# Attention and routed experts on one core: products without a reader ahead of the first expert's row transposes, and a new order for its first products

## The chip, the cores and the metric

The kernel runs on one core of one Trainium2 chip. The core has five engines with queues of their own: PE (TensorE, matrix products and transposes), DVE (VectorE), ACT (ScalarE), POOL (GpSimd) and SP (which here only issues transfers). An engine takes its instructions strictly in the order of its queue; a wait at the head holds back everything behind it. The profile also has PEld, the loading of a product's stationary operand, which overlaps PE. The metric is the device time of one execution in microseconds (us), less is better; the time before is the median of three runs.

## The reference

Two layers in a row. The first is an attention that adds a coarse part (queries, keys and values averaged by four, softmax over all) and a local part (softmax over the seven nearest keys). The second sends each of the 4608 tokens to one of 8 experts, greedily by score, 576 tokens to each, and applies that expert's two-layer network:

```
order = np.argsort(-flat)                 # all token-expert scores, highest first
for idx in order:
    tok, e = (int(idx) // E, int(idx) % E)
    if assigned[tok] >= 0 or counts[e] >= cap:
        continue
    assigned[tok] = e
    counts[e] += 1
...
for e in range(E):
    mask = assigned == e
    h = np.maximum(x[mask] @ w1[e], 0.0)  # 576 x 512 by 512 x 1024
    out[mask] = h @ w2[e]                 # 576 x 1024 by 1024 x 512
```

## The kernel before, in words

The attention comes first and takes about the first 292 us. It writes its rows x to memory and leaves the scores of all tokens on the chip. Then the experts follow one after the other, in the order in which they fill up. For each of them there are two parts.

*The routing* (class Routing, `phase`) finds the next expert to fill up and the list of its 576 tokens. It is a chain of comparisons on DVE (L703), counts on PE (L733, L744, L749) and small steps on DVE between them; `emit` turns the result into the list `idx`. Its last products are the 18 of L994; the list itself is written by four DVE instructions at L1004. The routing of the next expert is worked into the products of the current one: its setup on DVE (L810 to L856) is followed by the first comparison and count, and so on.

*The expert* (class Experts) loads its weights (`weights`, L1036), splits each of them into a high and a low 16-bit half (`split`: ACT makes the high one at L1052, DVE the low one at L1054), and gathers the 576 rows of x by five indirect transfers, issued by POOL (L1069): four row tiles of 128 rows and one of 64. For the first expert (and the second) each row tile is transposed on PE with four instructions (`piece`, L1078) into a bank of PSUM named pX, of which there are two; ACT copies it out as the high half of `xt` (L1081) and DVE subtracts to get the low half (L1082), which frees the bank. For the later experts a DMA transposes.

`mlp` does the products. The 1024 hidden columns are cut into eight blocks f of 128. For each of them the rows are cut in two: columns 0 to 255 of `xt` (row tiles 0 and 1) and columns 256 to 575 (row tiles 2, 3 and 4, 320 columns). Either part takes 12 products: four slices d of the depth, each with high by high, high by low and low by high halves. The order of the three matters here: the first product of a part only needs the high half of `xt`, the second needs the low half, which DVE makes last. Both parts of a block go to one tile pH in PSUM (two banks), of which there are two in turn; ACT takes it out with the rectifier (L1119), DVE makes the low half (L1122), and then the bank pair is free for block f + 2. The second layer's products (L1135) follow.

The order on each queue comes from the framework's planner. It takes instructions by priority as they become ready in its own estimate of times, so it may put a product of block 1 ahead of one of block 0 that still waits. The program can force an order: `issue_after` and `behind_` (L708) write an edge between two instructions of the same engine that sets their order in the queue and adds no wait. The routing and the first expert's row tiles are traced with the highest priority.

The queue of PE around the change, as the profile has it: 18 products of L994, the transposes of tiles 0 and 1, one product each of blocks 0 and 1, the transposes of tiles 2 and 3, ten products of block 0, the transposes of tile 4, the last of block 0's first part and most of block 1's first part, then block 0's 12 products of 320 columns and the rest of block 1's first part.

Of the kernel before, what the change touches and what calls it, by code (L numbers as in the profile page):

```python
# [6 lines left out]
F32 = mybir.dt.float32  # L7
# [1000 lines left out]
class Experts:  # L1008
    def __init__(self, ctx, tc, x_dram, w1, w2, out, ident, ps, raw):
        self.tc, self.nc, self.x, self.w1, self.w2, self.out, self.ps = tc, tc.nc, x_dram, w1, w2, out, ps  # L1010
        self.raw = raw
        self.wt = ctx.enter_context(tc.tile_pool(name="wt", bufs=2))
        self.wk = ctx.enter_context(tc.tile_pool(name="mwk", bufs=2))
        self.ident = ident
        self.sc, self.second, self.sent = [], {}, None

    def weights(self, ei, late):

        nc = self.nc
        raw = []  # L1020

        def load(eng, ii):
            e = eng.value_load(ei[:1, :1], min_val=0, max_val=E - 1)
            for i in ii:
                t = self.raw.tile([128, 2048], F32, name="nat")
                if i < 2:
                    src = self.w1[bass.DynSlice(e, 1), 256 * i:256 * i + 256].rearrange("o (a p) f -> p (o a) f", p=128)
                    dst = t.rearrange("p (a f) -> p a f", a=2)
                else:
                    src = self.w2[bass.DynSlice(e, 1), 512 * i - 1024:512 * i - 512].rearrange(  # L1030
                        "o (a p) d -> p (o a) d", p=128)
                    dst = t.rearrange("p (a d) -> p a d", a=4)
                n = dst.shape[1] // 2
                for a in ((0, n), (n, 2 * n)) if late and i < 2 else ((0, 2 * n),):
                    with self.tc.issue_after(self.sent.ins) if i > 1 and self.sent else nullcontext():
                        eng.dma_start(dst[:, a[0]:a[1]], src[:, a[0]:a[1]])  # L1036
                raw.append(t)

        load(nc.sync, (0, 1) if late else (0, 1, 2, 3))
        return (raw, lambda: load(nc.gpsimd, (2, 3))) if late else raw  # L1040

    def split(self, raw, first):

# [16 lines left out]
    def gather(self, idx, first):  # L1060


        nc = self.nc
        xt = self.wk.tile([128, 2, 4, CAP], F16, name="xt")
# [9 lines left out]
        def piece(c):  # L1074
            s0, n = SL[c]
            p = self.ps.tile([128, 4, 128], F32, name="pX", bufs=2)
            for d in range(4):
                self.turned = nc.tensor.transpose(p[:, d, :n], xgs[c][:n, 128 * d:128 * d + 128], self.ident[:n, :n])  # L1078
            hi, lo = xt[:, 0, :, s0:s0 + n], xt[:, 1, :, s0:s0 + n]
            with self.tc.high_priority():  # L1080
                nc.scalar.activation(hi, p[:, :, :n], AF.Copy, scale=XM)  # L1081
                nc.vector.scalar_tensor_tensor(lo, p[:, :, :n], XM, hi, op0=OP.mult, op1=OP.subtract)  # L1082
# [10 lines left out]

        return xt, piece if first else piece_dma

    def mlp(self, w, xt, idx, in1, in2):
        nc = self.nc

        ht = self.wk.tile([128, 8, 2 * CAP], F16, name="ht", bufs=1)
        CUT = ((0, 256), (256, CAP))  # L1100
        for f in range(8):
            p = self.ps.tile([128, 2, 512], F32, name="pH", bufs=2)
            seq = [(d, a, b) for d in range(4) for a, b in ((0, 0), (0, 1), (1, 0))]
            for s, (s0, s1) in enumerate(CUT):
                for j, (d, a, b) in enumerate(seq):
                    mm = nc.tensor.matmul(p[:, s, :s1 - s0], w[d][a][:, 128 * f:128 * f + 128], xt[:, b, d, s0:s1],  # L1106
                                          start=j == 0, stop=j == len(seq) - 1)
            if f == AFT:
                aft = mm
            with self.tc.high_priority():  # L1110
                los = []
                for i, (n0, n1) in enumerate(((0, 256), (256, 320))):
                    q = p[:, :, n0:n1] if i == 0 else p[:, 1:, n0:n1]
                    m = q.shape[1]
                    s0 = 0 if i == 0 else 512
# [9 lines left out]
        for c, (s0, n) in enumerate(SL):  # L1125
            p = self.ps.tile([128, 512], F32, name="pX", bufs=2)
# [3 lines left out]
            seq = [(h0, f, b) for f in range(8) for h0, b in ((s0, 0), (s0, 1), (lo, 0))]  # L1130
# [25 lines left out]
GET = {-1: (0, 1), 0: (2, 3), 1: (4,)}  # L1156
GET0 = {3: (0, 1), 4: (2, 3, 4)}
BEHIND = ((1, 6), (2, 10))


def moe_attention(tc, q, k, v, wg, w1, w2, cst, out):
    nc = tc.nc
    with ExitStack() as top:
# [6 lines left out]
        ro = Routing(top, tc, lg, cst)  # L1170
# [6 lines left out]
        with ExitStack() as ctx:  # L1177
# [3 lines left out]
            with tc.high_priority(TOP):  # L1181
                idx, (raw, rest) = ro.phase(False, True, lambda ei: ex.weights(ei, True))
                w, split = ex.split(raw, True)
                xt, piece = ex.gather(idx, True)
                with tc.issue_after(ex.fetched.ins):
                    rest()
                with tc.issue_after(ro.done.ins):
                    for k in range(4):
                        split(k)
                for c in range(5):  # L1190
                    piece(c)
            w1st = split
            for i in range(E):
# [32 lines left out]
                                    split(2 * c)  # L1226
                                    split(2 * c + 1)

                ex.mlp(w, xt, idx, in1, in2)
                if i == 0:  # L1230
                    for at, mms in zip(BEHIND, ro.late):
                        for mm in mms:
                            ro.behind_(mm, ex.second[at])
# [58 lines left out]
```

## Time and profile before

| | |
|---|---|
| median of 3 runs | 787.49 us (786.25 to 787.55) |
| the profiled execution's own time | 784.24 us |
| its span, from the first to the last instruction | 782.3 us |
| mean granted TensorE clock | 0.942 of full |
| PE busy | 676.3 us (86%) |
| DVE busy | 562.3 us (72%) |
| ACT busy | 331.8 us (42%) |
| POOL busy | 242.1 us (31%) |
| L1106, the first layer's products, high half of the weights: 1024, 287 ns each in the mean | 197.1 us |
| L1106, low half of the weights: 512, 287 ns each | 146.5 us |

The profile is of one execution, whose own time lies 3.25 us below the median. Its span is divided by engine, line and tile. [...] A transpose on PE is a matmul with the identity and stands under the line that issues it. PEclk is the clock that TensorE was granted, as a share of full speed: in the 40 slices of the page it is below full at nine places, the longest of them being slices 15 and 16 (about 293 to 332 us), where it is half. The share of busy time is a mean over stages; the change lies in one stage of some 20 us, so it is read from the windows and the timeline there.

### The profile page before, as it was taken

The page shows a single profiled execution, that of the slowest core. Times are in us where ns is not written, and L with a number is a line of the kernel's source. Part 1 is how long each engine was busy: PE and PEld are TensorE (multiplying, and loading weights), DVE is VectorE, ACT ScalarE, POOL GpSimd, SP SyncE. Part 2 cuts the span into 40 slices and gives each one's busy share as a digit, 9 for nine tenths or more (in the row PEclk, how much of TensorE's full clock was granted, in tenths as well). Part 3 has the DMA queues.
Part 4 walks back from the last instruction along what each step waited for, and adds up shares of the span by engine and source line. Part 5 has one row for each costly group of instructions (what it writes and reads, how often), then busy time and mean ns, then how long its engine had stood idle before and what let it go on. Part 6 is the DMA issues. An engine that isn't in the chain of part 4 may idle for free.

```text
span 782.3 us, 21188 instructions
## 1 busy us (share of the span) xinstructions
PE 676.3 (86%) x8565; PEld 467.8 (60%) x8565; DVE 562.3 (72%) x1679; ACT 331.8 (42%) x631; POOL 242.1 (31%) x274
## 2 busy tenths in 40 slices
PE   6588888986988873399899999999989999999994
PEld 4577677775777662265466466466457476574752
DVE  7778878987797887886968979798959645171210
ACT  3357576673766450341623426134225234262210
POOL 9263544735355450300510412121230402201001
PEclk9689999998999995599999999999999999999997
DMA  9949979797999850620714565562742673804001
GB/s 262 217 121 246 249 197 268 199 271 195 260 229 206 204 184 12 182 96 27 277 34 163 168 137 208 102 238 61 227 171 108 131 267 75 216 2 101 22 27 34
DMA packets 148133, 125.00 MB, mean 160 GB/s; under 512 B 92228, under 2 KB 122436, under 8 KB 148036
## 3 DMA queue, kind: packets, MB, share of 16 engines
q1 hardware_dynamic: 140656, 102.12, 49.2%
q0 software_dynamic: 6432, 20.98, 8.9%
q8 instruction: 68, 1.11, 0.6%
q10 hardware_dynamic: 948, 0.55, 0.3%
q14 instruction: 29, 0.24, 0.1%
HBM read 95.30 MB, written 21.23 MB: 149 GB/s over the span
## 4 chain that ended last, share of the span: by engine, by line
PE 33%; issue 26%; DVE 22%; DMA 7%; ACT 5%; POOL 3%; SPq 2%; another core or an unknown queue 1%; ACTq 0%; POOLq 0%; DVEq 0%
PE pH L1106 8%; PE pX L1135 6%; PE g L476 2%; POOL out_dram L1144 2%; DMA vw<-in_v_dram 2%; DVE cmp L703 2%; PE g L292 2%; PE pR L733 2%; PE g L325 2%; PE g L436 2%; PE g L373 1%; DVE x L407 1%; PE g L454 1%; DVE wl L1054 1%; DVE xt L499 1%
## 5 line engine op out<-in xcount | busy, mean ns | idle before, releaser
L1106 PE MATMUL pH<-xt,wh 128*128 128x256 f16 (+1 forms) x1024 | 197.1, 287 | 0.7 <-ACT xt L1081 0.7
L1135 PE MATMUL pX<-wh,ht 128*128 128x512 f16 (+1 forms) x640 | 182.2, 383 | 1.9 <-DVE xt L1082 1.9
L1106 PE MATMUL pH<-xt,wl 128*128 128x320 f16 (+1 forms) x512 | 146.5, 287 | 0.0
L1135 PEld LDWEIGHTS <-ht 128*128 128x128 f16 (+1 forms) x960 | 82.1, 101 | 91.5 <-issue 7.8
L1144 POOL DMA_INDIRECT out_dram<-y,idx x40 | 44.4, 1111 | 286.4 <-ACT y L1141 262.4
L1135 PE MATMUL pX<-wl,ht 128*128 128x512 f16 (+1 forms) x320 | 119.1, 384 | 0.0
L1106 PEld LDWEIGHTS <-wh 128*128 128x128 f16 x1024 | 97.8, 98 | 26.7 <-issue 3.5
L1119 ACT ACTIVATE ht<-pH 128x512 f16<-128x512 f32 (+1 forms) x128 | 45.5, 408 | 123.3 <-PE pH L1106 123.3
L1054 DVE SCALAR_TENSOR_TENSOR wl<-nat,wh 128x512 f16<-128x512 f32 x128 | 84.7, 683 | 2.7 <-ACT wh L1052 0.5
L1069 POOL DMA_INDIRECT xg<-x_dram,idx x40 | 47.1, 1178 | 105.2 <-DVE idx L1004 34.0
L1141 ACT ACTIVATE y<-pX 128x512 f32<-128x512 f32 (+1 forms) x40 | 23.7, 593 | 130.5 <-PE pX L1135 78.5
L1122 DVE SCALAR_TENSOR_TENSOR ht<-pH,ht 128x512 f16<-128x512 f32 (+1 forms) x128 | 52.5, 450 | 33.8 <-ACT ht L1119 33.3
L1052 ACT ACTIVATE wh<-nat 128x1024 f16<-128x1024 f32 x64 | 66.6, 1056 | 9.9 <-DMA nat<-in_moe_w_dram 9.9
L1106 PEld LDWEIGHTS <-wl 128*128 128x128 f16 x512 | 50.1, 98 | 11.9
L465 ACT COPY pt<-g 64x512 f32<-64x512 f32 x72 | 41.8, 580 | 33.7 <-PE g L454 32.5
L292 PE MATMUL g<-ident,nat 128*128 128x128 f32 x256 | 41.1, 288 | 13.7 <-DMA nat<-in_q_dram 8.7
L476 PE MATMUL g<-vw,pt 128*64 128x65 f32 x1152 | 45.0, 231 | 5.6 <-issue 3.0
L1143 DVE SCALAR_TENSOR_TENSOR y<-pX,y 64x512 f32<-64x512 f32 x8 | 5.5, 693 | 59.8 <-ACT y L1141 59.8
L476 PEld LDWEIGHTS g<-vw,pt 128*64 128x64 f32 x1152 | 39.9, 144 | 11.6 <-ACT pt L465 5.6
L278 ACT COPY kt<-g 64x512 f32<-64x512 f32 (+1 forms) x56 | 35.2, 629 | 19.4 <-PE g L292 11.6
L278 ACT COPY qz<-g 64x512 f32<-64x512 f32 (+1 forms) x52 | 33.0, 635 | 21.2 <-PE g L292 20.6
L265 POOL TENSOR_TENSOR gtmp<-qz 64x576 f32<-64x576 f32 x28 | 32.0, 1144 | 30.8 <-DVE kdt L268 29.2
(219 smaller groups left out, 1189.5 us busy)
## 6 DMA issues: line engine op xcount, KB each, us to landing
nat<-in_moe_w_dram SPq DMA_DIRECT2D x28, 1024.0 KB
vw<-in_v_dram SPq DMA_DIRECT2D x136, 96.0 KB
up<-up_dram SPq DMA_DIRECT2D x36, 256.0 KB
x_dram<-x SPq DMA_DIRECT2D x36, 256.0 KB
nat<-in_q_dram SPq DMA_DIRECT2D x16, 512.0 KB
nat<-in_k_dram SPq DMA_DIRECT2D x16, 512.0 KB
nat<-in_v_dram SPq DMA_DIRECT2D x14, 512.0 KB
up_dram<-xu SPq DMA_DIRECT2D x16, 128.0 KB
```

The source lines that it names most:

```text
L278: self.nc.scalar.copy(out, in_)
L292: nc.tensor.transpose(p[:, a, :, fp], src[:, 4 * hh + 2 * a + s, 2 * fp:2 * fp + 2].rearrange("p f d -> p (f d)"), self.ident)
L465: self.nc.scalar.copy(out, in_)
L476: nc.tensor.matmul(o[64 * i:64 * i + 64, 65 * h:65 * h + 65], pt[:, 2 * g + i, h].rearrange("p b q -> p (b q)"), self.vw[u % 4][:, i, 4 * ...
L1052: nc.scalar.activation(hi, r, AF.Copy, scale=sc)
L1054: nc.vector.scalar_tensor_tensor(lo[:, a:a + LOP], r[:, a:a + LOP], sc, hi[:, a:a + LOP], op0=OP.mult, op1=OP.subtract)
L1069: self.fetched = nc.gpsimd.indirect_dma_start(out=xg[:n], out_offset=None, in_=self.x, in_offset=bass.IndirectOffsetOnAxis(ap=idx[:n, c:c ...
L1106: mm = nc.tensor.matmul(p[:, s, :s1 - s0], w[d][a][:, 128 * f:128 * f + 128], xt[:, b, d, s0:s1], start=j == 0, stop=j == len(seq) - 1)
L1119: last = nc.scalar.activation(hi, q, AF.Relu)
L1122: nc.vector.scalar_tensor_tensor(lo, q, 0.0, hi, op0=OP.max, op1=OP.subtract)
L1135: mm = nc.tensor.matmul(p[o:o + m], ht[:, f, h0:h0 + m], w[4 + f // 2][b][:, 512 * (f % 2):512 * (f % 2) + 512], start=j < parts, stop=j > ...
L1144: i = nc.gpsimd.indirect_dma_start(out=self.out, in_=y[:n], in_offset=None, out_offset=bass.IndirectOffsetOnAxis(ap=idx[:n, c:c + 1], axis=0))
```

## The change

Three edits, all for the first expert only.

1. `spin` issues 24 products right behind the last product of L994 (an `issue_after` edge). Each multiplies a tile of ones (128 by 128, 16 bit) with a table of 288 columns that the routing keeps on the chip, and writes to a pH tile that nobody reads.
2. In `mlp` the first parts (256 columns) of blocks 0 and 1 are issued ahead of the second part of block 0, so that the first 24 products need row tiles 0 and 1 alone. For the other blocks, and the other experts, the order is as it was.
3. Order edges put the transposes of row tile 2 behind product 6 of those 24 (counted from 0), those of tile 3 behind product 12, those of tile 4 behind product 18.

```diff
+    def spin(self, a, b):
+        p = self.ps.tile([128, 2, 512], F32, name="pH", bufs=2)
+        n = b.shape[1] * b.shape[2]
+        for _ in range(SPIN):
+            self.nc.tensor.matmul(p[:, 0, :n], a, b.rearrange("p e t -> p (e t)"), start=True, stop=True)
+
...
+            self.turns.append([])
             for d in range(4):
                 self.turned = nc.tensor.transpose(p[:, d, :n], xgs[c][:n, 128 * d:128 * d + 128], self.ident[:n, :n])
+                self.turns[-1].append(self.turned)
...
-    def mlp(self, w, xt, idx, in1, in2):
+    def mlp(self, w, xt, idx, in1, in2, first=False):
...
+        seq = [(d, a, b) for d in range(4) for a, b in ((0, 0), (0, 1), (1, 0))]
+
+        def product(f, p, s):
+            s0, s1 = CUT[s]
+            for j, (d, a, b) in enumerate(seq):
+                mm = nc.tensor.matmul(p[:, s, :s1 - s0], w[d][a][:, 128 * f:128 * f + 128], xt[:, b, d, s0:s1],
+                                      start=j == 0, stop=j == len(seq) - 1)
+                self.products.append(mm)
+            return mm
+
+        ph = {}
         for f in range(8):
-            p = self.ps.tile([128, 2, 512], F32, name="pH", bufs=2)
-            seq = [(d, a, b) for d in range(4) for a, b in ((0, 0), (0, 1), (1, 0))]
-            for s, (s0, s1) in enumerate(CUT):
-                for j, (d, a, b) in enumerate(seq):
-                    mm = nc.tensor.matmul(p[:, s, :s1 - s0], w[d][a][:, 128 * f:128 * f + 128], xt[:, b, d, s0:s1],
-                                          start=j == 0, stop=j == len(seq) - 1)
+            for z in (0, 1) if first and f == 0 else () if first and f == 1 else (f,):
+                ph[z] = self.ps.tile([128, 2, 512], F32, name="pH", bufs=2)
+                product(z, ph[z], 0)
+            p = ph.pop(f)
+            mm = product(f, p, 1)
...
+TURN = (6, 12, 18)
+SPIN = 24
...
+                with tc.issue_after(ro.late[-1][-1].ins):
+                    ex.spin(ro.one, ro.codes)
...
-                ex.mlp(w, xt, idx, in1, in2)
+                ex.mlp(w, xt, idx, in1, in2, i == 0)
                 if i == 0:
+                    for at, mms in zip(TURN, ex.turns[2:5]):
+                        for mm in mms:
+                            ro.behind_(mm, ex.products[at])
```

More of the change, by code (lines that the diff above doesn't have):

```diff
@@ L1014, in __init__ @@
         self.ident = ident
-        self.sc, self.second, self.sent = [], {}, None
+        self.sc, self.second, self.sent, self.products, self.turns = [], {}, None, [], []
     def weights(self, ei, late):
```

## The prediction

> **What bounds the kernel now.** I read the stage table first (busy us of PE, PEld, DVE, ACT, POOL, each with its count; then granted clock, DMA share, GB/s), then the chain of waits, then the clock.
>
> ```profile
> span 782.3 us, 21188 instructions
> 320.20:326.10 5.90, 0.00 (x0) 0.00 (x0) 5.68 (x21) 3.17 (x3) 3.28 (x3) 0.50 0.57 208
> 337.50:350.70 13.20, 12.60 (x121) 8.80 (x120) 11.85 (x30) 6.66 (x13) 0.00 (x0) 1.00 0.01 2
> 350.70:385.00 34.30, 34.30 (x256) 18.40 (x256) 27.47 (x109) 11.18 (x19) 6.38 (x6) 1.00 0.44 157
> ```
>
> After the first expert's list of tokens PE is idle for 5.90 us, at half clock. From 350.70 to 385.00 it has no gap, so what is won or lost at 350.70 reaches the end. From 337.50 to 350.70 both PE (12.60 of 13.20) and DVE (11.85) are nearly full. The chain between, in order of time (start, length, what; pieces of 0.05 us and less left out):
>
> ```profile
> 322.21 3.92 DMA xg<-x_dram,idx
> 326.18 1.13 PE pX L1078 x4
> 327.33 0.60 ACT xt L1081
> 327.93 1.16 issue
> 329.09 0.61 ACT xt L1081
> 329.74 0.58 PE pH L1106 x2
> 330.32 1.79 PE pX L1078 x8
> 332.10 2.03 PE pH L1106 x10
> 334.13 0.41 PE pX L1078 x4
> 334.56 0.39 ACT xt L1081
> 334.98 0.42 DVE xt L1082
> 335.41 0.09 DVE h L829
> ...
> 337.02 0.84 DVE cmp L703
> 337.90 0.42 PE pR L733 x10
> ```
>
> Row tile 0 is transposed when its gather lands (326.13), tile 1 when its own lands (327.93). Two products follow ACT's copy of tile 1; DVE's subtraction frees the rest, and the planner has filled that wait with tiles 2 and 3. That subtraction ends at 329.72 + 0.69 = 330.41:
>
> ```profile
> 329.72 0.69 DVE L1082 SCALAR_TENSOR_TENSOR xt<-pX,xt 128x512 f16<-128x512 f32 x1 [1.06 <-ACT xt L1081]
> ```
>
> Behind tile 4's subtraction stands DVE's setup for the second expert, whose comparison ends at 337.85.
>
> **The clock.** Rows of the granted clock (length, PE busy, count, clock, DMA share, GB/s). Each of these holds a change:
>
> ```profile
> 292.75:293.00 0.25, 0.00 (x0) 0.87 0.00 0
> 333.80:333.90 0.10, 0.10 (x3) 0.53 1.09 451
> 388.50:389.00 0.50, 0.00 (x0) 0.51 0.00 0
> 391.50:392.00 0.50, 0.50 (x6) 0.58 0.81 319
> ```
>
> A row's mean clock places the change in it: 0.87 in 292.75 to 293.00 is a fall at 292.94; the others are at 333.89 (rise), 388.51 (fall) and 391.92 (rise). The distances are 40.95, 54.62 and 3.41 us: 12, 16 and 1 times 3.413. So the clock is decided on a grid of 3.413 us. Six stretches of that grid, in the same columns:
>
> ```profile
> 289.52:292.93 3.41, 1.63 (x32) 1.00 0.39 144
> 74.48:77.89 3.41, 1.80 (x42) 1.00 0.30 92
> 770.80:774.21 3.41, 1.31 (x14) 1.00 0.20 77
> 327.07:330.48 3.41, 2.09 (x10) 0.50 0.68 197
> 388.51:391.92 3.41, 2.89 (x14) 0.50 0.22 74
> 47.17:50.58 3.41, 3.41 (x40) 0.50 0.00 0
> ```
>
> I laid that grid over the whole span. It falls nine times; the busiest stretch ahead of a fall is 1.63 of 3.41 (48%), the idlest after which it stayed full is 1.80 (53%). It rose after 2.89 (85%), not after 2.09 (61%), and once not after a full one. I take: below about half busy it falls; above some 61 to 85% it rises.
>
> **The change, part by part.**
>
> ```profile
> 318.61 1.42 PE L994 MATMUL pR<-r,ohl 128*64 128x72 bf16 x18 [2.85 <-DVE r L981]
> 332.11 0.42 PE L1106 MATMUL pH<-xt,wl 128*128 128x256 f16 x1
> 332.75 0.42 PE L1106 MATMUL pH<-xt,wl 128*128 128x256 f16 x1
> 336.11 0.30 PE L1106 MATMUL pH<-xt,wl 128*128 128x320 f16 x1
> 336.52 0.30 PE L1106 MATMUL pH<-xt,wl 128*128 128x320 f16 x1
> 337.17 0.38 PE L1106 MATMUL pH<-xt,wh 128*128 128x256 f16 x2
> 337.39 0.27 PE L1106 MATMUL pH<-xt,wl 128*128 128x256 f16 x1
> 386.50 0.66 PE L1078 MATMUL pX<-ident,xg 128*128 128x128 f32 x4 [0.98 <-ACT y L1141]
> 389.03 0.58 PE L1135 MATMUL pX<-wh,ht 128*64 128x512 f16 x1 [1.87 <-DVE xt L1082]
> ```
>
> Prices from start to start: a product of 256 columns is 0.64 / 3 = 0.213 us at half clock (three from 332.11 to 332.75) and 0.22 / 2 = 0.11 at full (two from 337.17 to 337.39). One of 320 is 0.41 / 3 = 0.137 at full. Four transposes are 1.13 at half (chain) and 0.65 at full (386.50).
>
> *The 24 products* have 288 columns, so 0.24 us at half, 0.122 at full. They follow L994's last product (320.03). Were the clock never to rise they end at 320.05 + 5.76 = 325.81, before the gather at 326.13: hidden in the idle 5.90 us. Without that cover they would cost 2.9 to 5.8 us. They write a pH buffer that nobody reads; its next user is PE itself, so no wait comes of it. On the recorded grid the stretch 320.24 to 323.65 is full: the clock rises at 323.65, with 15 done; the nine left take 1.1 us, to 324.75.
>
> *What of the clock is left.* Stretch 323.65 to 327.07 holds 1.1 + 0.65 (tile 0) = 1.75, 51%: between 48 and 53%, undecided; I take it as kept. Tile 1 is gated by its gather and gains 1.13 − 0.65 = 0.48: the first two products start at 329.26, the rest at 329.94 (the subtraction, 0.48 earlier). Stretch 327.07 to 330.48 then holds 0.65 + 0.3 + 0.54 = 1.5, 44%: **the clock falls again at 330.48**, just as the products become dense, and rises at 333.89 as before. A fall one step earlier only takes the 0.48 away.
>
> *The moved transposes*, on PE. By 330.48 some 7 products are done. At half clock follow one more (0.28), tile 2 (1.13), five products (1.07) and most of tile 3 by 333.89; then its end (0.1), six products (0.65), tile 4 (0.41, to 335.05) and five products (0.54): 335.6. Tile 4's subtraction lasts ACT's 0.39 and DVE's 0.42 with about 0.1 of gaps, to 336.0, and the second product of 320 columns waits for it, some 0.3. Eleven of them (1.5) end at 337.5. Before, the same 36 products and five transposes ended at 337.39 + 0.11 = 337.50. So PE's sum is 0.0: the 0.48 goes into waits that tiles 2 and 3 filled before.
>
> *ACT and DVE.* The moved transposes issue no DMA; ACT's copies and DVE's subtractions move with them on those queues. ACT has room (1.16 us of issue between two copies in the chain). On DVE it matters: tile 4's subtraction ends at 336.0 instead of 335.40, and what is queued behind it (L829 to the comparison, then PE's count L733) would be 0.6 late. If the planner, seeing tile 4 later, puts the setup ahead of it, that chain comes up to 0.6 early instead. At the end of the stage DVE has slack:
>
> ```profile
> 350.70 0.17 DVE L751 TENSOR_REDUCE nj<-pR 128x1 f32<-128x8 f32 x1 [0.87 <-PE pR L749]
> ```
>
> It waits 0.87 us for PE there, so a late DVE costs only through the waits that it makes for PE before: between 0 and +0.6. The subtotal is −0.6 to +0.6.
>
> *The grid of other executions.* Nothing in one execution ties the grid to the kernel's start. Shifted by −0.8, +0.8, +1.7 and +2.3 us, the same working has the clock fall again at 326.3, 327.9, 328.8 and 325.9, and PE ends its 36 products 0.6, 2.1, 0.4 and 0.6 us later than before on the same grid. With the recorded grid's 0.0 the middle one of the five is +0.6. PE's waits in the next stage (13.20 − 12.60 = 0.60) can take up a little of it; I take **+0.5 us**. On the profiled execution's own 784.24 (span 782.3 and 1.94 around it) that is 784.7. This execution is 3.25 below the median of 787.49; on the median it is 788.0. The case's own range is −0.6 (recorded grid, DVE early) to +2.1.
>
> [...]
>
> **The rivals.**
>
> *The clock stays full* (a lower limit than half, or a luckier grid). Then the first two products start at 329.26, five or so follow from 329.94 to 330.6, tile 2 to 331.27, products, tile 3 to 332.46, products, tile 4 from 333.1 to 333.5, the 24 end at 334.0, a wait to 334.45 for the subtraction, and the 320s end at 336.0: PE −1.5, DVE −0.95. (Tile 4's gather is there: tile 3's had landed by about 331.2, amid the eight transposes of the chain, and two gathers landed 1.8 us apart, 326.13 and 327.93.) The change is between these, −1.25: 786.2. For it: after the spin no gap exceeds 1.4 us, and the undecided stretch lies at the limit. Against it: nine falls of nine below 48%, one of them at 38% (1.31 of 3.41).
>
> *Slower: the rise comes a grid step late.* Before, tiles 2 and 3 keep PE full from 329.74 on; now PE must pass seven products before tile 2, and idles until the subtraction (about 0.3 us at half clock). It decides where the grid puts a boundary near 331.3: before, that stretch (327.87 to 331.28) holds 1.13 + 1.54 = 2.67, 78%; now 1.13 + 0.4 + 0.83 = 2.4, 70%. Both lie between 61 and 85%; with the limit between them, the half clock lasts 3.41 us longer, which costs PE up to 1.7, and with the 0.3 lost and DVE's chain behind it +2.0: 789.5. For it: the rows leave the limit open just there. Against it: it needs a grid in about a third of the positions.
>
> *It does nothing*: the planner finds no place for the products ahead of tile 0, or orders the later transposes as now. Then 787.5. Against it: both are bound by written order edges.
>
> **How the numbers follow.** 0.2% is 1.57 us, about what a measurement of this kernel can tell from no change. Chances: forecast 0.47, clock stays full 0.32, late rise 0.16, nothing 0.05. New orders on DVE and ACT farther on, which no row shows, can add some to either side. Faster: half of the second (its own bound of −1.5 is just short), 0.16, and an eighth of the first, 0.06: 0.22. Slower: four fifths of the third, 0.13, and a sixth of the first, 0.08: 0.21. Same: 0.57. The range reaches from a little beyond the clock kept (−2.1, 785.4) to the late rise (+2.1, 789.6).
>
> **What would show it.** Right: clock 1.00 from about 323 to 326, 0.50 again somewhere between 326 and 333, products of 0.213 us among the transposes. Wrong: a clock of 1.00 from 324 to 338 (the first rival), a tile 0 that starts after 326.3 (the spin costs), the first comparison for the second expert ending more than 1 us from 337.85 (the order on DVE changed), or a shift at 337 that is not the shift at 385.

## The result, and the profile after

The changed kernel takes 785.09 us (median of 22 runs, 782.21 to 796.54) beside 788.59 for the kernel before (22 runs on the same chip). The ratio is 0.9943, with a 95% interval of 0.9924 to 0.9963: it is faster by some 4.5 us. (The ratio is that of the mean times, without the slow run of 796.54 us, 1.8% above the fastest.) The profiled execution took 783.15 us. Forecast were 788.0 and a range from 785.4 to 789.6.

From the page of the changed kernel, the head, the busy times and one of the DMA queues (packets, MB, share of 16 engines):

```profile
span 781.4 us, 21233 instructions
PE 681.5 (87%) x8589; PEld 471.6 (60%) x8589; DVE 560.8 (72%) x1679; ACT 332.0 (42%) x631; POOL 245.5 (31%) x274
q8 instruction: 68, 1.11, 0.6%
```

PE is busy 5.2 us longer than before (676.3) and still the kernel is shorter. The queue of instructions is as before, 68 packets; it will matter below.

The timeline of PE in the changed kernel (start, length, work, count, idle time ahead and its releaser). New line numbers: 1046 the added products, 1085 the transposes (1078 before), 1114 and 1153 the products of the first and second layer (1106, 1135).

```profile
320.19 1.42 PE L994 MATMUL pR<-r,ohl 128*64 128x72 bf16 x18 [2.85 <-DVE r L981]
321.54 5.07 PE L1046 MATMUL pH<-codes,one 128*128 128x288 bf16 x24
327.84 0.66 PE L1085 MATMUL pX<-ident,xg 128*128 128x128 f32 x4 [1.23 <-DMA xg<-x_dram,idx]
329.42 0.66 PE L1085 MATMUL pX<-ident,xg 128*128 128x128 f32 x4 [0.92 <-DMA xg<-x_dram,idx]
330.76 0.38 PE L1114 MATMUL pH<-xt,wh 128*128 128x256 f16 x2 [0.69 <-issue]
332.14 1.04 PE L1085 MATMUL pX<-ident,xg 128*128 128x128 f32 x8
385.41 0.66 PE L1085 MATMUL pX<-ident,xg 128*128 128x128 f32 x4 [0.36 <-ACT y L1159]
387.94 0.38 PE L1153 MATMUL pX<-wh,ht 128*64 128x512 f16 x1 [1.87 <-DVE xt L1090]
```

The added products end 1.23 us ahead of tile 0, which the gather releases 7.65 us after the first L994 product (327.84 − 320.19; before 7.57): they are hidden. The clock, in windows of the changed kernel (length, busy us of PE, PEld, DVE, ACT, POOL with counts; granted clock, DMA share, GB/s):

```profile
325.50:325.75 0.25, 0.25 (x4) 0.14 (x3) 0.25 (x2) 0.19 (x1) 0.13 (x1) 0.84 0.00 0
325.58:328.99 3.41, 1.69 (x12) 1.01 (x10) 3.41 (x7) 1.49 (x2) 2.76 (x3) 1.00 0.54 154
328.99:332.41 3.42, 1.95 (x15) 1.53 (x16) 2.54 (x6) 0.74 (x2) 3.11 (x4) 1.00 0.72 193
571.34:574.75 3.41, 1.40 (x17) 1.01 (x18) 1.15 (x3) 0.59 (x1) 1.30 (x1) 1.00 0.53 193
```

The first row places the rise at 325.58, in the added products, and in this execution the clock stays full until 574.75: the first whole stretch of the grid behind the rise held 1.69 of 3.41 us, half. The last row is the stretch ahead of that later fall, 41% busy. The chain of waits of the changed kernel has the first comparison for the second expert far earlier than before:

```profile
335.40 0.74 DVE cmp L703
336.19 0.41 PE pR L733 x10
```

It ends 15.95 us after the first L994 product (336.14 − 320.19), where it ended 19.25 after it before (337.86 − 318.61). On DVE the setup for the second expert now stands ahead of the subtractions of tiles 2 to 4, not behind that of tile 4.

Where did the time go? Marks of the two profiles, in us after the first L994 product, worked out from the timelines of PE:

```
                                       before   after   gained
second layer of expert 1 starts         44.0     42.4     1.6
second layer of expert 1 ends           74.6     70.5     2.5 more
PE ends                                453.5    451.0    -1.6 more
```

The first stage gains 1.6, the next 2.5, and the rest gives 1.6 back. The clock fall at 574.75 (6.8 us at half clock) lies in that rest; a second profile of the change (e4 below), without a fall there, needs 377.3 us for it, where the kernel before needs 378.9 (453.5 − 74.6). So some 1.6 us were gained there too, where no line of the program changed.

### The profile page after: what moved, and what is told of

Read it like the earlier page. It is cut to its first block, busy times and chain, and to the rows that moved or that the text cites. A ratio compares the mean times of both kernels' runs of the same rounds, so it can differ in the third digit from the quotient of the medians.

```text
span 781.4 us, 21233 instructions
## 1 busy us (share of the span) xinstructions
PE 681.5 (87%) x8589; PEld 471.6 (60%) x8589; DVE 560.8 (72%) x1679; ACT 332.0 (42%) x631; POOL 245.5 (31%) x274
## 3 DMA queue, kind: packets, MB, share of 16 engines
q8 instruction: 68, 1.11, 0.6%
## 4 chain that ended last, share of the span: by engine, by line
PE 33%; DVE 26%; issue 21%; DMA 10%; ACT 4%; POOL 3%; SPq 2%; POOLq 0%; DVEq 0%; ACTq 0%
PE pH L1114 9%; PE pX L1153 7%; DMA vw<-in_v_dram 3%; DVE wl L1060 3%; PE pR L733 2%; POOL out_dram L1162 2%; DVE cmp L703 2%; DMA up<-up_dram 2%; PE g L292 2%; PE g L476 2%; DVE ht L1140 2%; PE g L436 1%; PE g L325 1%; DMA nat<-in_q_dram 1%; DMA nat<-in_k_dram 1%
## 5 line engine op out<-in xcount | busy, mean ns | idle before, releaser
L1162 POOL DMA_INDIRECT out_dram<-y,idx x40 | 46.2, 1154 | 280.5 <-ACT y L1159 258.4
L1075 POOL DMA_INDIRECT xg<-x_dram,idx x40 | 49.0, 1225 | 105.3 <-DVE idx L1004 34.7
```

Source lines behind the costliest of these rows:

```text
L1075: self.fetched = nc.gpsimd.indirect_dma_start(out=xg[:n], out_offset=None, in_=self.x, in_offset=bass.IndirectOffsetOnAxis(ap=idx[:n, c:c ...
L1162: i = nc.gpsimd.indirect_dma_start(out=self.out, in_=y[:n], in_offset=None, out_offset=bass.IndirectOffsetOnAxis(ap=idx[:n, c:c + 1], axis=0))
```

## What the experiments asked

None of these kernels leaves out a part of the computation; they add, drop or move products without a reader, and the order. Three theories are named in the expectations: A, the clock decides; B, the new order and DVE's setup decide; S, the added products act as instructions, since they shift what comes behind them on PE. All marks below are us after the first L994 product of the profile in question, and "order" says that the 24 first products and transposes stand in the order of the change. The shift is in PE instructions (a product and its weight load are two: 8589 of each on the page above).

```
run                    shift order   median   before  ratio   95% interval
e1_spin_only             48   old    787.34   790.55  0.9976  0.9944 1.0007
e2_order_only             0   new    788.06   790.55  0.9983  0.9951 1.0015
e3_clock_held            74   new    785.31   790.55  0.9953  0.9920 0.9986
e4_change_again          48   new    784.23   790.55  0.9947  0.9918 0.9977
e5_cold_products         48   old    780.95   783.01  0.9978  0.9951 1.0005
e6_change_12_wide        24   new    781.97   783.01  0.9988  0.9966 1.0009
e7_order_cold            48   new    780.73   783.01  0.9989  0.9962 1.0015
e8_before_again           0   old    784.37   783.01  1.0010  0.9990 1.0031
e9_held_between          72   new    776.30   780.83  0.9944  0.9919 0.9969
e10_change_thrice        48   new    776.98   780.83  0.9955  0.9935 0.9975
e11_12_wide_12_small     48   new    777.82   780.83  0.9969  0.9940 0.9997
e12_held_everywhere      98   new    776.26   780.83  0.9924  0.9897 0.9951
```

Each group of four shares a chip. The times alone part few of these; the profiles do. The marks, one profile for each kernel (when the clock was at half among the first products, when expert 1's second layer starts and ends, and how long it is from there to PE's end):

```
run                    half clock     2nd layer  its last  from there
                       in products    starts     product   to PE's end
before                 to 15.3        44.0       74.6      378.9
after                  none           42.4       70.5      380.5 (6.8 us at half clock)
e1_spin_only           11.5 to 18.3   44.8       73.9      379.9 (6.8 us at half clock)
e2_order_only          to 14.2        43.6       73.3      380.6 (3.4 us at half clock)
e3_clock_held          none           43.1       72.9      378.4 (3.4 us at half clock)
e4_change_again        9.2 to 16.0    44.3       72.4      377.3
e5_cold_products       to 14.8        43.7       74.0      372.1
e6_change_12_wide      7.9 to 14.7    43.8       73.6      374.6
e7_order_cold          to 14.6        43.7       73.5      372.4
e8_before_again        to 14.5        43.7       76.2      374.3
e9_held_between        10.2 to 13.6   43.0       71.1      372.4
e10_change_thrice      10.1 to 16.9   44.4       72.5      372.8
e11_12_wide_12_small   10.2 to 17.0   44.5       72.6      372.6
e12_held_everywhere    none           42.4       70.5      372.9
```

The last column can be compared within a chip and between profiles with the same clock falls. On the chip of e5 to e8, with no fall in that part, it is 374.3 and 374.6 for shifts of 0 and 24 (e8, e6) against 372.1 and 372.4 for 48 (e5, e7). On the chip of e1 to e4, with one fall of 3.4 us each, it is 380.6 for a shift of 0 (e2) against 378.4 for 74 (e3).

### The parts alone, and the change once more

e1 has the added products and the order of before, e2 the new order without them:

```diff
# e1: mlp is called as before, and TURN's edges are gone
-                ex.mlp(w, xt, idx, in1, in2, i == 0)
+                ex.mlp(w, xt, idx, in1, in2)
...
# e2: no added products
-                with tc.issue_after(ro.late[-1][-1].ins):
-                    ex.spin(ro.one, ro.codes)
# e3: the clock held through the gaps behind tiles 0 and 1
+HOLD = (8, 5)
...
+                    if c < 2:
+                        with tc.issue_after(ex.turned.ins):
+                            ex.spin(ro.one, ro.codes, HOLD[c])
```

> The 24 products alone, with the order of the first expert's products and transposes as before. Theory A (the clock that stays full through the first products is the gain): faster by 1.5 to 3 us (ratio about 0.997), granted clock 1.00 in the stretch in which the first products run, and the list of the second expert about 1.5 us earlier counted from the first L994 product. Theory B (the new order is the gain, because DVE's setup for the second expert no longer stands behind the later tiles' subtractions): within 0.7 us of before (ratio 0.999 to 1.001), although the clock is full.

> The new order of products and transposes alone, without the 24 products. Theory A: no gain, or a loss of up to 1 us (ratio 0.999 to 1.002), since the first products run at half clock as before. Theory B: faster by 2 to 4 us (ratio about 0.996).

> The whole change, with 8 more products of the same kind behind the transposes of tile 0 and 5 more behind those of tile 1, so that the idle stretches in which the clock could fall are filled. If the clock's fall on unlucky grids still costs the change part of its gain, this is faster than the change by 0.5 to 1 us (ratio to before about 0.993); if the clock plays no part, it is as the change or slower by up to 0.5 us (the first product may wait for the added ones).

> The change itself once more, beside the others on the same chip, with a second profile: the ratio again near 0.994 (0.991 to 0.997). Theory A expects the clock to be 1.00 between 8 and 20 us after the first L994 product in most executions; the forecast expected it to fall to 0.50 in there.

Each part alone gains 0.2% or so, which its interval can't tell from nothing. e1's 0.9976 is near A's 0.997, but its interval reaches into B's 0.999 to 1.001; e2's 0.9983 lies between A's and B's values, and its interval holds values of both. So the times decide nothing between A and B. In e1 the clock, once risen, fell again in the middle of the dense products and the second layer started 0.8 us later than before; yet the execution got ahead later. e4 is the change in an execution in which the clock falls as the prediction had it. Windows of e4, columns as above:

```profile
327.01:330.43 3.42, 1.50 (x11) 0.84 (x9) 3.42 (x7) 1.05 (x2) 2.81 (x3) 1.00 0.66 167
330.43:333.84 3.41, 2.32 (x10) 1.53 (x11) 1.85 (x4) 0.60 (x1) 2.77 (x4) 0.50 0.78 195
333.84:337.25 3.41, 3.41 (x18) 2.88 (x17) 2.79 (x12) 1.45 (x4) 0.00 (x0) 0.50 0.86 310
```

The first stretch is full clock and 44% busy, and the next is at half: the fall is where the prediction put it, behind as many busy us as it had there (1.5 of 3.41). The second stretch, 68% busy, didn't bring the rise; the third did. The second layer then starts at 44.3, 0.3 later than before. So with a falling clock the first products gain nothing, and with a kept one (after, e3, e12) they start the second layer at 42.4 to 43.1. Both agree with the prediction. But the change as it is, whose clock falls in some executions, does not come out slower than e3, which keeps it by force (0.9947 and 0.9953; the intervals leave room for some us either way). What happens to the clock in the first products does not explain the whole gain, since part of it arises after expert 1, where no instruction changed.

### The shift

From the end of expert 1 on, the profiles of before and after have the same instructions of PE, DVE, ACT and POOL in the same order. What can still differ is where in PE's stream the packets of the instruction queue fall: the page's queue q8 moves 68 packets, 1.11 MB, 16.3 KB each, and 17130 products and weight loads of PE (2 x 8565) by 68 are some 250 for each. Counted in the trace's records of DMA packets and of PE, the 26 packets behind the added products come, in the changed kernel, 46 products and weight loads earlier in the program in the median (43 in the mean, standard deviation 23); the 24 products and their loads are 48. The 42 ahead of them stand 2 later in the median. I read these packets as fetches of blocks of PE's instructions, on these counts alone, and call each a fetch below.

Windows of the kernel before, 131 us after its first L994 product, in the row transfers of the third expert (the last two columns are DMA share and GB/s):

```profile
449.00:449.50 0.50, 0.50 (x5) 0.31 (x5) 0.50 (x2) 0.00 (x0) 0.00 (x0) 1.00 1.10 208
450.00:450.50 0.50, 0.50 (x5) 0.26 (x6) 0.50 (x2) 0.23 (x1) 0.00 (x0) 1.00 3.81 70
450.50:451.00 0.50, 0.50 (x7) 0.11 (x1) 0.14 (x2) 0.37 (x1) 0.00 (x0) 1.00 0.08 9
```

A share of 3.81 with 70 GB/s says that the packets which began there lasted long (they are counted where they begin; 25 of them took 0.95 to 1.24 us); behind it the engines hardly begin any, 0.08. PE pays some 4 us later, in the timeline of the kernel before, and again in the fourth expert's turn:

```profile
454.07 0.29 PE L733 MATMUL pR<-ol,cmp 128*128 128x32 bf16 x5 [1.16 <-DVE cmp L703]
502.00 0.29 PE L733 MATMUL pR<-ol,cmp 128*128 128x32 bf16 x5 [1.66 <-DVE cmp L703]
```

The places of the fetches (from the trace's DMA records) against the row transfers of experts 3 and 4:

```
run                    shift  transfers      fetch   transfers      fetch
before                   0    128.6-136.4    130.9   176.2-184.2    178.4
e2_order_only            0    127.4-135.2    130.3   175.3-183.2    177.4
e8_before_again          0    130.3-138.3    132.8   177.8-185.7    179.9
e6_change_12_wide       24    127.7-136.3    129.7   175.5-183.4    177.7
after                   48    125.4-133.1    124.5   172.6-180.2    171.8
e1_spin_only            48    128.7-136.4    127.7   175.8-183.4    175.0
e4_change_again         48    126.9-134.7    125.9   174.2-181.7    173.2
e5_cold_products        48    128.0-135.6    126.9   174.8-182.4    173.8
e7_order_cold           48    127.6-135.3    126.5   174.6-182.2    173.7
e11_12_wide_12_small    48    127.0-134.7    126.2   173.9-181.5    173.1
```

With a shift of 0 or 24 both fetches fall inside the transfers, with 48 some 1 us ahead of them. The time of a fetch does not follow the shift evenly: e6's came 2.0 us behind the start of the transfers, where its expectation has 0.7. The four kernels that test this:

```diff
# e5 (order of before) and e7 (order of the change): 24 products of 8 columns, the clock at half until 14.8 and 14.6
...
-            self.nc.tensor.matmul(p[:, 0, :n], a, b.rearrange("p e t -> p (e t)"), start=True, stop=True)
+            self.nc.tensor.matmul(p[:32, 0, :8], a[:, :32], b[:, 0, :8], start=True, stop=True)
# e6: 12 products of 512 columns
-SPIN = 24
+SPIN = 12
...
+            self.nc.tensor.matmul(p[:, 0], a, a[:, None].to_broadcast([128, 4, 128]), start=True, stop=True)
# e11: as e6, and 12 products of 8 columns behind them
+        for _ in range(SPIN):
+            self.nc.tensor.matmul(p[:32, 1, :8], a[:, :32], b[:, 0, :8], start=True, stop=True)
```

> The order of before, with 24 products in the place of the change's 24, but of 8 columns and with 32 columns of weights: PE's stream is 48 instructions longer from there on, as in the change, and the clock stays at half when the first products run. Theory S (the 48 instructions shift the places at which PE's 16 KB instruction blocks are fetched, so that the fetches no longer fall into the row transposes by DMA of the third and fourth expert): the DMA share shows no slice above 2 at 131 and 178 us after the first L994 product, the waits of PE there (1.2 and 1.7 us) are gone or halved, and the kernel is 1.5 to 2 us faster than before (ratio about 0.998). Theory A (only the clock counts): as before (0.999 to 1.001), with both stalls present.

> The change with 12 products of 512 columns in place of 24 of 288: 5.1 us at half clock instead of 5.8, so the same clock, but a shift of 24 instructions instead of 48. The third and fourth expert's fetches would then fall about 0.7 us behind the start of the DMA transposes (2.2 behind it without a shift, 0.9 ahead of it with 48). Theory S: the stalls and waits of before come back, and it is 1.5 to 2 us slower than the change (ratio to before about 0.997). Theory A: as the change (ratio 0.994).

> The new order of the change, with the 24 small products of 8 columns: everything of the change but the clock. Its distance to the change is what the clock is worth: theory A some 2 to 3 us (ratio to before 0.998), theory S about 1 us or less (ratio to before 0.995 to 0.996), since the shift (about 1.8 us) and the order (about 1.3 us) remain.

> The kernel before itself, for a second profile and the spread of the comparison: ratio 0.998 to 1.002; the two DMA stalls at 131 and 178 us after the first L994 product again (theory S), and the granted clock falling at the end of the first expert in some executions and not in others.

e5 and e7 have no clock from the added products (half until 14.8 and 14.6, as before) and still run 372.1 and 372.4 us behind the first expert, against 374.3 of the kernel before: 2.0 us. e6, which has the order of the change and 12 added products in place of 24, runs 374.6. e6 and e7 share a chip and differ in nothing but those products: the queues of DVE, ACT and POOL and the rest of PE's are the same in order. So it is the shift, and not the new order, that this part answers to.

The times say less. Of e5 against e8, the kernel before run among these four, the difference of the means is −3.4 ± 2.0 us; against the 35 runs of the kernel before beside them e5's interval (0.9951 to 1.0005) just reaches 1. e6 (order and clock, without the fetches' move) has 0.9988, as theory S expected (0.997) rather than A (0.994). e7 is a miss of S: it expected 0.995 to 0.996, and A 0.998; measured were 0.9989, with an interval (0.9962 to 1.0015) that holds A's value and not S's. So S, which left about 1 us or less to the clock, had the clock too small. Neither the shift nor the clock alone carries the gain of the change.

> The change with 12 products of 512 columns, as in the run of that name, and 12 more of 8 columns behind them: the same added busy time within 0.4 us and the same order, but a shift of 48 instructions in place of 24. S: the fetches of PE's instruction blocks move from inside the row transfers of the third and the fourth expert to just ahead of them (126 and 173 us after the first L994 product, against 129.7 and 177.6), the two slices of DMA stall and the two waits of 1.3 to 1.5 us at L733 go, and the time comes out 2.0 us below that of the 12 wide products alone, a ratio of 0.996 to the kernel before. Rival (only the clock and the order count): as the 12 wide products alone, a ratio of 0.9988, and the stalls stay.

e11 shows it from the other side: against e6 all queues but PE's are the same in order, PE's has 12 small products more, and the clock falls in both. It ran on another chip than e6; e10, the change on e11's chip, has 372.8 in the last column, beside 372.1 and 372.4 of the same shift on e6's, so the chips differ little there. Timelines of e6 (the row transfers, ACT's copy, DVE's subtraction, PE's count in the third and in the fourth expert's turn):

```profile
449.21 8.62 SPq L1098 DMA_TRANSPOSE xt<-xs  x5
454.18 0.63 ACT L1095 ACTIVATE xs<-xg 64x512 f16<-64x512 f32 x1 [1.32 <-DMA xt<-xs]
454.84 0.68 DVE L1096 SCALAR_TENSOR_TENSOR xs<-xg,xs 64x512 f16<-64x512 f32 x1 [1.38 <-ACT xs L1095]
456.21 0.29 PE L733 MATMUL pR<-ol,cmp 128*128 128x32 bf16 x5 [1.32 <-DVE cmp L703]
504.05 0.29 PE L733 MATMUL pR<-ol,cmp 128*128 128x32 bf16 x5 [1.47 <-DVE cmp L703]
```

and the DMA queues of e6 from 450.9 to 451.9, with its windows:

```profile
q1 hardware_dynamic: 748, 0.19, 107.8%
q8 instruction: 1, 0.02, 7.5%
```

```profile
451.00:451.50 0.50, 0.50 (x5) 0.30 (x5) 0.50 (x2) 0.00 (x0) 0.00 (x0) 1.00 1.24 239
451.50:452.00 0.50, 0.50 (x4) 0.12 (x2) 0.46 (x3) 0.00 (x0) 0.00 (x0) 1.00 3.48 137
452.50:453.00 0.50, 0.50 (x7) 0.11 (x1) 0.12 (x2) 0.35 (x1) 0.00 (x0) 1.00 0.08 9
```

The instruction packet lies among the transfers of q1; the stall follows. The staging buffer xs comes free late, ACT's copy waits 1.32 us for a transfer, DVE's subtraction 1.38 for ACT, the comparison stands behind it on DVE, and PE waits 1.32 us. The same rows of e11, and its DMA queues from 444.2 to 445.2:

```profile
445.38 7.68 SPq L1100 DMA_TRANSPOSE xt<-xs  x5
448.92 0.62 ACT L1097 ACTIVATE xs<-xg 64x512 f16<-64x512 f32 x1
449.57 0.68 DVE L1098 SCALAR_TENSOR_TENSOR xs<-xg,xs 64x512 f16<-64x512 f32 x1
450.99 0.29 PE L733 MATMUL pR<-ol,cmp 128*128 128x32 bf16 x5
497.87 0.29 PE L733 MATMUL pR<-ol,cmp 128*128 128x32 bf16 x5
```

```profile
q8 instruction: 1, 0.02, 6.0%
q0 software_dynamic: 1, 0.00, 1.0%
```

The instruction packet is out ahead of the transfers, these last 7.68 us in place of 8.62, and no wait is left. The fourth expert's turn repeats it (1.47 us at L733 in e6, none in e11), and the stage after expert 1 goes from 374.6 to 372.6. The time's ratio, 0.9969, lies between the two expectations (0.996 and 0.9988) and its interval holds both; the verdict rests on the profile. The single packets tell the same: the median packet of q1 in the row transfers lasts 0.018 us. With a fetch inside the transfers 20 to 28 of them, the first begun 0.2 to 0.6 us behind the fetch, last up to 1.24 to 1.63 us and end together (before, e2, e6, e8); with the fetch ahead of them (e4, e11) none lasts over 0.54.

Two limits belong to this. In these traces a fetch inside dense transfers cost PE time only where somebody waited for them soon: in e6 a third fetch, 341.7 us after the first L994 product in the seventh expert's transfers, was followed within 0.2 us by 23 packets of over 0.6 us, and PE has no wait of over 0.9 us behind it. And long packets are not the fetch's alone: in other places of the traces groups of up to 18 of them stand with no fetch in the 2.5 us ahead, but with 65 or more packets of q0 (the indirect transfers) about them; in the eight cases of the third and fourth expert no packet of q0 is there.

### The step to the second expert, and a faster kernel

```diff
# e9: 12 more products without a reader ahead of the last row tile of the second layer (e12: e3 and this)
+                        if c == 3:
+                            with tc.issue_after(ex.turned.ins):
+                                ex.spin(ro.one, ro.codes, BETWEEN)
```

> The change, with 12 more products without a reader in the gap of 1.87 us that PE has before the last row tile of the first expert's second layer (behind the transposes of the second expert's row tiles 0 and 1). S (the added products gain by where they put the fetches of PE's instruction blocks, 2.0 us, and by the clock where the grid allows it): the clock is kept at 1.00 through the step from the first to the second expert, where it fell in six of ten profiles; that is worth 1.7 us in an execution that falls and nothing in one that doesn't, so 0.5 to 1.2 us below the change on the same chip; the fetches stay ahead of the transfers of the third and fourth expert (72 instructions of shift). Rival (what the clock loses there lies beside DVE's work): the clock is kept and the second layer of the second expert ends no earlier, 0.0 from the change.

> The kernel with the change, for a comparison on this chip. All theories: 3 to 4.5 us below the kernel before (ratio 0.9943 to 0.9962). From the end of the first expert's second layer to PE's end: S 372 to 379 us by the clock falls that it meets, and no wait of over 1 us at L733 in the third and the fourth expert's turn.

> The change, with 8 and 5 products without a reader behind the transposes of row tiles 0 and 1, and 12 in the gap ahead of the last row tile of the second layer. S: clock of 1.00 from about 4 us after the first L994 product through the second expert's first layer in every execution; second layer started at 43.1 or earlier, first expert's end at 72.5, no stalls at 131 and 178; 1 to 2 us below the change on the same chip, a ratio of 0.992 to 0.994. Rival (the shift of 98 instructions puts another fetch into a transfer): a wait of over 1 us at L733 or at a row transfer that the change lacks, and a time equal to the change's.

Between the start of expert 1's second layer and its end the marks fall in groups. With the order of before and a clock fall of one step of the grid 30.3 and 30.6 (e5, before), of two steps 32.5 (e8), without a fall 29.1 (e1); with the new order and a fall 29.8 (e2, e3, e6, e7), without a fall 28.1 (after, e4, e10, e11). So the order is worth 0.5 to 0.9 there, and a fall costs 1.2 to 1.7 (of 3.4 us at half clock). In the ten profiles before e9 the clock fell there in seven; the expectation of e9 has six. The order's part shows in PE's wait for ACT's y ahead of the second transposes: 0.98 before (the row of 386.50), 0.36 after. The timeline of e12 at that place:

```profile
383.44 0.66 PE L1085 MATMUL pX<-ident,xg 128*128 128x128 f32 x4 [0.36 <-ACT y L1159]
383.93 1.63 PE L1046 MATMUL pH<-codes,one 128*128 128x288 bf16 x12
385.97 0.38 PE L1153 MATMUL pX<-wh,ht 128*64 128x512 f16 x1 [0.40 <-DVE xt L1090]
```

The gap of 1.87 is filled and the clock kept in e9 and e12; in e10, the change beside them, it happened to be kept too, and there the filling gains nothing (28.1 in all three). On the mean times e9 is −0.4 ± 1.9 us from the change (expected −0.5 to −1.2), e12 −2.0 ± 2.1 (expected −1 to −2). e10 is as expected (0.9955, 372.8, no wait of over 1 us at L733). e12 is at or ahead of the marks that were expected of it (42.4 for 43.1, 70.5 for 72.5, no stalls) and has the lowest ratio of all, 0.9924, but that it beats the change isn't shown.

### The shares

A fit over 241 executions of the twelve experiments and of the kernel before beside them gives 0.22 ± 0.05 us for each us at half clock, −1.4 ± 0.7 for the shift and −0.6 ± 0.7 for the order (95%; 2.2 us scatter left). It has a constant for each chip, the time at half clock of each execution, taken as 2 x (1 − mean granted clock) x span, and a term each for a shift of 48 or more and for the new order. The change had 88.4 us at half clock (e4) against 98.0 before (standard error 1.2 each): −9.6 x 0.22 = −2.1. Together −4.1, beside −3.5 to −4.5 of the three comparisons (0.9955, 0.9947, 0.9943). The order's term alone is not told from nothing. The clock's −2.1 is an estimate: its price of 0.22 comes from the scatter between executions, most of whose half clock lies elsewhere in the kernel, and no experiment sets that time alone.

## Why the prediction was wrong, step by step

**The 24 products.** Their time is hidden, as forecast (tile 0 not later by more than 0.1 us), and the rise comes inside them. The step that failed is their price. "Without that cover they would cost 2.9 to 5.8 us" is the only one the working gives them: they were counted as time on PE and as activity for the clock. As 48 instructions in PE's stream they were put at nothing, without a reason. They move the fetch of two blocks out of the row transfers of experts 3 and 4 and save 2.0 us (372.1 and 372.4 in e5 and e7 against 374.3 and 374.6 in e8 and e6), a term that the sum lacks. The page of before has the row of q8 (68 packets, 1.11 MB), and its timeline the waits of 1.16 and 1.66 at L733; they lie over 110 us behind the change, and the working did not use them.

**"From 350.70 to 385.00 it has no gap, so what is won or lost at 350.70 reaches the end."** It does, but the working took the reverse with it, that nothing else would be won or lost, apart from a clause that new orders farther on "can add some to either side". The prediction's own last sign, a shift at 337 that is not the shift at 385, appeared: the first comparison came 3.3 us earlier, the second layer 1.6.

**What of the clock is left.** In the first products the working held, and the two outcomes were about right in size. Kept: the prediction's first rival had −1.5 for PE, measured −1.6 at the start of the second layer (after) and −0.9 and −1.6 (e3, e12, which force it). Falling: 0.0, or +0.5 over the grids; measured +0.3, +0.4, +0.5 and −0.2 (e4, e10, e11, e6). At the place that the working itself used, the last of the 36 first products, it was less good: it starts 1.0 earlier than before in after and e12 and 0.3 earlier in e3 (forecast −1.5), and with a fall 0.9, 1.0, 1.0 and 0.4 later in e4, e10, e11 and e6 (forecast 0.0 to +0.6 for most grids). The profile after shows the sign that the prediction named for its first rival, a clock of 1.00 throughout (from 325.58); e4 shows the likeliest case. Which outcome came differed between executions of the same kernel (kept in after, a fall in e4 and e10): in the nine profiles in which added products had raised the clock, it was kept after stretches of 1.69 and more (after, e3, e12) and fell after 1.51 and less (the other six). For its first rival the prediction had that no gap behind the spin exceeds 1.4 us. That did not keep the clock: it fell in e4 at 330.43 with no gap above 1.2 us ahead; the longest, in e4's timeline:

```profile
330.69 1.12 PE L1085 MATMUL pX<-ident,xg 128*128 128x128 f32 x4 [1.17 <-DMA xg<-x_dram,idx]
```

The late rise of the slower rival is real (68% busy did not bring it), but the second layer then started 0.3 later, not 2.0.

The limit of about half, read from one profile, does not hold over the whole span in the others. Stretches at the end of the attention were followed by a fall although they were busier, up to 69%, and a stretch of 45% was followed by none (the first row is of e11, the second of e4, both at full clock):

```profile
287.59:291.00 3.41, 2.34 (x43) 2.03 (x41) 2.90 (x10) 2.07 (x4) 1.97 (x2) 1.00 0.58 213
388.46:391.87 3.41, 1.54 (x14) 1.10 (x16) 3.41 (x6) 2.70 (x4) 3.11 (x2) 1.00 0.08 22
```

In e11 the clock is at half from 291.00, in e4 it stays full to 774.16. The grid of 3.413 us holds in all fourteen profiles; what is compared with what limit on it is open.

**What is missing of the clock** is the rest of the kernel's time at half clock: the change lowers it by 9.6 us in the mean, of which the fit makes 2.1 us (an estimate, as said), while the working weighed the grid up to 337 only. Part of it may lie at the step from expert 1 to 2, where the new order leaves PE 0.6 us less idle. In the profiles with the new order and no product in that gap the clock fell there in four of eight (not in after, e4, e10, e11), with the old one in three of four (not in e1); whether the order makes that fall rarer is open.

**ACT and DVE.** "If the planner, seeing tile 4 later, puts the setup ahead of it" was the right branch, but up to 0.6 early was too small: the setup passed tiles 2 and 3 too, and the comparison came 3.3 us early. At the end of the first expert the new order is worth about 0.7; that it comes from the earlier comparison is not shown, and that the forecast's −0.6 for that branch has about this size is luck.

**The forecast and the range.** The working up to the second layer was right to about a us, averaged over the outcomes. The likeliest case lacked −2.0 (fetch) and −0.7 (order at the next step), which would have put it at 785.3. The measured ratio of 0.9943 makes 783.0 of the 787.49 that the forecast stands on; the 2.3 us between are about what the fit gives the clock. "Faster" got 0.22 because no rival contained an effect behind 385.

## What to carry to other kernels

Adding instructions to an engine can also move later packets of the instruction queue against everything else, as here (46 products and loads in the median for 48 added on PE; from some 2 us behind the start of the third and fourth experts' transfers to some 1 us ahead of it): look for these packets in the profile, see whether one lies inside a run of dense small DMA transfers with a reader close behind, and try the same kernel with a few dozen cheap instructions more or less before a gain is put down to what they compute. A change at one place is to be followed to the end of the trace with marks from a common start, since what differs where no line changed is a mechanism of its own. For the clock, look at the busy share of each stretch of its grid, not only at the longest gap (e4 fell with none above 1.2 us); but take a limit that one profile shows as a hint, since other profiles of the same kernel break it.

## What was not expected of the hardware

- With one instruction packet of 16.3 KB among the row transfers, 20 to 28 packets of q1, the first begun 0.2 to 0.6 us behind its start, lasted up to 1.24 to 1.63 us, beside a median of 0.018, and hardly any began until they ended (in before a DMA share of 0.08 or less); with the packet ahead of the transfers none lasted over 0.54. Why they last so long isn't shown.
- The clock was kept at 49.6% busy (1.69 of 3.41) and fell at 44% and 41% (1.50, 1.40); it did not rise after 68%. It also fell early in the profile after, behind a stretch of 51%:

```profile
8.14:11.55 3.41, 1.74 (x14) 1.27 (x13) 2.76 (x4) 2.44 (x4) 3.35 (x4) 1.00 1.06 290
```

  With the rows of 69% and 45% above, the profile's modelled busy time gives no sharp limit.
- An us at half clock cost 0.22 us in the mean of the fit. At the two places that the profiles price it was about half: up to 1.7 for 3.4 us at the step to the second expert, 3.2 for 6.8 (after against e4) from 574.75 on. That the mean is lower because PE is idle in much of its half clock, as from 320.20 to 326.10 before, is likely but not measured.
